# Settled engine orders, one more chunk in token order, and a shorter TensorE warm-up in a two-layer linear-attention kernel

## The chip, the cores and the metric

The kernel runs on one core of one Trainium2 chip. The metric is the device time of one execution in microseconds (us); smaller is better. A profile comes from one execution whose span (first to last instruction) is some 1.7 us shorter than the device time of the same run.

## The reference, cut to what matters

Two identical layers, each an attention block A and an MLP block B, over 2048 tokens of width 512; 32 heads of 16; hidden width 1792; everything in bf16.

```python
def _A_ref(x, wqkv, wo):                       # x: (1, 2048, 512)
    qkv = (x @ wqkv) ...                       # split in q, k, v by heads
    phi = lambda t: jnp.where(t > 0, t + 1, jnp.exp(t)) + 1e-6
    pq, pk = phi(q), phi(k)
    kv  = einsum("bhsd,bhse->bhde", pk, v)     # sums over ALL tokens
    z   = einsum("bhsd->bhd", pk)              # sums over ALL tokens
    num = einsum("bhqd,bhde->bhqe", pq, kv)
    den = einsum("bhqd,bhd->bhq", pq, z)[..., None] + 1e-6
    return (num / den) ... @ wo

x = x + _A_ref(_layernorm(x), wqkv, wo);  x = x + _B_ref(_layernorm(x), w1, b1, w2, b2)
x = x + _A_ref(_layernorm(x), wqkv, wo);  x = x + _B_ref(_layernorm(x), w1, b1, w2, b2)   # [cut]
```

What matters: kv and z need every token, so each layer has a **join** at which nothing of the attention's output can start until the last phi(k) has been summed. The kernel hides it behind Q tiles and behind the other block.

## The kernel before

The kernel is a list of named operations. Each has an engine, a modelled duration, the data that it reads and writes, and the buffers ("tiles") that it takes. A scheduler in the kernel file puts the operations of each engine in one order when the kernel is built; the engine's program holds them in that order, and semaphores do the waiting.

The names used below: `K0_9` is the K tile of token tile 9 in layer 0 (the code counts layers from 0, the text of the prediction from 1), `Q0_1_2` a Q tile of chunk 1 (four token tiles make a chunk), `G` the sums of phi(k) with the normed input y, from which the kv product is made, `Z` the sums of phi(k), `D` the denominator matmul, `KV`, `M` the products at the join, `WO` the attention's output, `PTA` a transpose on TensorE, `TA` one by DMA; `stats`, `aggr`, `veps`, `pow`, `norm` are the steps of a layer norm (`pow` on POOL), `exp`, `relu`, `min`, `phi` those of phi.

Before, the order came out of priorities. Among the operations that could start soon, the one with the smallest number went first:

```python
def run(self):                                       # class Scheduler, before
    ...                                              # [cut]
        for o in released[e]:
            at = max(o.ready, t0)
            pr = o.prio
            if o.table is not None and o.table != table:     # [shortened]
                at = max(o.ready, t0 + TABLE_LOAD)
                pr += self.table_penalty
            ...                                      # [cut: a free buffer or bank?]
            if at <= t0 + self.window ...:           # the best priority among those that start soon
                if soon is None or (pr, at, o.seq) < soon[:3]:
                    soon = (pr, at, o.seq, o)
    ...
CONF = dict(N_K=4, N_Q=2, ..., TABLE_PENALTY=25.46, WINDOW=126.58,
    SHIFT={"B00_0": -359.6, "B00_1": -532.9, ...,    # [cut: some 260 tuned numbers]
           "phik0_2": 27.1, "phik1_8": 23.4, ...},
    WAY={..., "den0_2": "tok", "den1_2": "tok", "den1_3": "tok", ...})   # free choices
```

The kernel uses PSUM (the memory that TensorE writes to) as eight banks of 128x512 fp32. They are given out by the same scheduler, by its modelled times: whichever allowed bank is free first is taken.

```python
def take(self, t):                                   # class Banks
    _, b = min(self.options(t))                      # earliest free bank, in modelled time
```

The denominators of a chunk can be made in two ways. In the usual one TensorE multiplies phi(q) with a block matrix `zb`, ACT takes Ln and Exp (a reciprocal), and DVE or POOL multiplies. In the **token form** Q comes out with tokens on the partitions; DVE or POOL multiplies by z, DVE sums over each head's 16 columns and takes the reciprocal, and a DMA transpose turns the result round:

```python
if by_token(L, c):                                   # WAY["den{L}_{c}"] == "tok"
    for k in range(4):
        G.op("pool" or "dve", ... tensor_tensor(lr, tok(), zrow, mult) ...)      # pz
        G.op("dve",  ... tensor_reduce(rd, heads(lr), X, ADD) ...)               # red
        G.op("dve",  ... rd + 1e-6 ...)                                          # den
        G.op("dve",  ... reciprocal(rr, rd) ...)                                 # rec
        G.op("pool" or "dve", ... tok() * rr ...)                                # pr
        dma("sp", ... dma_start_transpose(...))                                  # TP
    return pt
for kt in range(DT):
    G.op("pe",  ... matmul(bank(b), lhsT=zb[...], rhs=pq[:, kt, :]) ...)         # D
    G.op("act", ... Ln, then Exp(scale=-1) ...)                                  # ln, rec
    G.op("pool" or "dve", ... pq * lr ...)                                       # pr
```

The warm-up keeps TensorE busy while the first input arrives:

```python
def warm(e):
    for _ in range(11):
        ins = e.matmul(bank(wu), lhsT=onesm[:, 0:P], rhs=onesm[:, :], start=True, stop=True)
    return ins
```

Of the kernel before, what the change touches and what calls it, by code (L numbers as in the profile page):

```python
# [22 lines left out]
ENGINES = ("pe", "act", "dve", "pool", "sp")  # L23
# [29 lines left out]
class Op:  # L53
    __slots__ = ("eng", "fn", "dur", "lat", "deps", "tiles", "prio", "name", "table", "sem", "nbytes",
                 "idx", "start", "end", "ready", "missing", "outs", "waits", "tok", "opens", "seq", "fast", "n", "grp", "soft")

    def __init__(self, eng, fn, dur, lat, prio, name, table=None, sem=None, nbytes=0, fast=False, n=1):
# [6 lines left out]

        self.soft = []
# [47 lines left out]
class Scheduler:  # L113


    def __init__(self, graph, psum, table_penalty=4.0, window=60.0):
        self.g = graph
        self.psum = psum
        self.table_penalty = table_penalty
        self.window = window  # L120
# [6 lines left out]
    def run(self):  # L127
        g = self.g
        for o in g.ops:
            o.soft = [d for d in o.soft if d not in o.deps]  # L130
            o.missing = len(o.deps) + len(o.soft)
        for o in g.ops:
            for d in [*o.deps, *o.soft]:
                d.outs.append(o)
        released = {e: [] for e in ENGINES}
        for o in g.ops:
            if o.missing == 0:
                released[o.eng].append(o)
# [6 lines left out]
        left = len(g.ops)  # L145
        while left:
            best = None
            for e in ENGINES:
                cand = None
                t0 = free[e]  # L150
                soon, late = None, None
                for o in released[e]:
                    at = max(o.ready, t0)
                    pr = o.prio
                    if o.table is not None and table is not None and o.table != table:
                        at = max(o.ready, t0 + TABLE_LOAD)
                        pr += self.table_penalty
                    ok = True
                    for t in o.tiles:
                        if t.slot is None:  # L160
                            s = self.slot_time(t)
                            if s is None:
                                ok = False
                                break
                            if s > at:
                                at = s
                    if not ok:
                        continue
                    if at <= t0 + self.window or (o.table is not None and at <= t0 + TABLE_LOAD + self.window and o.table != table):
                        if soon is None or (pr, at, o.seq) < soon[:3]:  # L170
                            soon = (pr, at, o.seq, o)
                    if late is None or (at, pr, o.seq) < late[:3]:
                        late = (at, pr, o.seq, o)
                if soon is not None:
                    cand = (soon[1], soon[0], soon[3])
                elif late is not None:
                    cand = (late[0], late[1], late[3])
                if cand is not None and (best is None or cand[:2] < best[:2]):
                    best = cand
            if best is None:  # L180
                raise RuntimeError("no operation can start: " + str(
                    [(e, [o.name for o in released[e]][:6]) for e in ENGINES]))
            at, _, o = best
# [30 lines left out]
            released[e].remove(o)  # L214
            left -= 1
# [4 lines left out]
            for w in o.outs:  # L220
                w.missing -= 1
                if o not in w.soft:
                    w.ready = max(w.ready, o.end + self.latency(o, w))
                if w.missing == 0:
                    released[w.eng].append(w)
# [70 lines left out]
def assign_waits(graph, order, sems, dma_sems):  # L296
# [10 lines left out]
    while len(done) < total:  # L307
# [45 lines left out]
    N_HALF=1, N_K=4, N_Q=2, P_Z0=0.37, N_PB=1, N_PT=8, P_DEN=-3.16, P_A2=-51.68, P_W1=-4.93, P_W2=79.13,  # L353
    P_K=87.88, P_G=146.7, P_Q=46.72, STEP=1.68, A1_Q=81.1, A1_STEP=4.54, N_H=2, N_N=2, GAP=0,
    TABLE_PENALTY=25.46, WINDOW=126.58,
    SHIFT={
        "B00_0": -359.6, "B00_1": -532.9, "B00_2": 40.9, "B00_3": 41.9, "B01": 316.2, "B02": 368.2,
        "B03": 123.2, "B10_0": -153.5, "B10_1": -88.2, "B10_2": 8.8, "B10_3": 74.2, "B11": 335.0,
        "B12": 293.5, "B13": -86.9, "D00": -322.6, "D01": -51.3, "D02": -123.2, "D03": 13.2, "D10": 4.8,
        "D11": -31.4, "D12": -41.2, "D13": 102.5, "G00_0": -22.1, "G00_1": -11.3, "G00_2": 110.8,  # L360
        "G00_3": 221.9, "G01_0": -39.6, "G01_1": 112.5, "G01_2": -42.7, "G01_3": -305.4, "G02_0": 213.7,
        "G02_1": -30.8, "G02_2": 606.6, "G03_0": -23.0, "G03_1": -78.8, "G03_3": -25.3, "G0_2_0": 12.2,
        "G10": -239.1, "G11": 116.2, "G12": 664.9, "G13": -18.0, "G1_1_0": -8.3, "G1_3_0": 17.0, "K00_0": 1.2,
# [98 lines left out]
def build_kernel(nc, A_x, A_wqkv, A_wo, B_x, B_w1, B_b1, B_w2, B_b2, out, conf=None, report=False):  # L462
# [5 lines left out]
    with ExitStack() as es:  # L468
# [131 lines left out]
        def warm(e):  # L600
            for _ in range(11):
                ins = e.matmul(bank(wu), lhsT=onesm[:, 0:P], rhs=onesm[:, :], start=True, stop=True)
            return ins
# [629 lines left out]
```

## Time and profile before

| | before |
|---|---|
| device time, median of the first 3 runs | 334.51 us (333.75 to 335.18) |
| span of the profiled run | 332.2 us |
| TensorE busy | 324.7 us |
| DVE, ACT, POOL busy | 219.1, 208.7, 146.8 us |
| TensorE gaps and late clock after 1.5 us | about 6.3 us |

A busy TensorE hides small gaps, so the useful measure is the distance from the start of one matmul to the next, less what the same shape takes in the steady part (the prediction below works these distances out). Whatever is above that is a **gap**. All gaps in this document are made in this way, and single ones under 0.1 us are mostly left out.

### The profile page before, as it was taken

What the parts mean: (1) busy time and instruction counts of PE and PEld (TensorE: products, weight loads), DVE (VectorE), ACT (ScalarE), POOL (GpSimd) and SP (SyncE); (2) the same over time, 40 slices, a digit from 0 to 9 for tenths busy, and PEclk for the clock granted to TensorE, in tenths of its full rate; (3) what the DMA queues carried; (4) which work ended last, traced back from release to release, by engine and by line L of the source; (5) the groups of instructions that cost most, each with busy time, mean ns of one, the idle gap of its engine ahead of it and who ended that gap; (6) DMA issues with size and microseconds to landing.
All of it is one profiled execution on the core that took longest, in us unless ns stands there. A gap on an engine that the chain in (4) does not pass through costs nothing.

```text
span 332.2 us, 4772 instructions
## 1 busy us (share of the span) xinstructions
PE 324.7 (98%) x1735; PEld 159.6 (48%) x1735; DVE 219.1 (66%) x461; ACT 208.7 (63%) x348; POOL 146.8 (44%) x238
## 2 busy tenths in 40 slices
PE   7999899999999999999999999999999999999996
PEld 3444444487444444444444444448744444444444
DVE  6988669996974593060777889998898585520022
ACT  2988499598989739374562286979956501735600
POOL 5883415768862938020359400284793062120000
DMA  7745750122030102122010110001152122201011
GB/s 264 258 76 83 258 190 0 34 47 49 17 79 2 33 0 39 26 47 49 16 32 3 32 33 2 0 17 34 39 116 69 32 66 64 47 15 35 0 40 57
DMA packets 42836, 19.07 MB, mean 57 GB/s; under 512 B 36476, under 2 KB 41852, under 8 KB 42812
## 3 DMA queue, kind: packets, MB, share of 16 engines
q1 hardware_dynamic: 39244, 11.55, 16.1%
q0 software_dynamic: 1056, 4.72, 4.0%
q10 hardware_dynamic: 2512, 2.49, 2.3%
q8 instruction: 14, 0.23, 0.3%
q14 instruction: 10, 0.08, 0.1%
HBM read 8.00 MB, written 2.10 MB: 30 GB/s over the span
## 4 chain that ended last, share of the span: by engine, by line
PE 78%; DVE 9%; DMA 5%; POOL 4%; ACT 3%; issue 1%; DVEq 0%; POOLq 0%
PE ps L1030 27%; PE ps L992 26%; PE ps L960 8%; PE ps L717 4%; PE ps L748 3%; PE ps L844 3%; DMA t<-yb 3%; PE ps L735 2%; PE ps L812 2%; POOL rstd L630 2%; DMA b1t<-b1r 1%; DVE gtb L828 1%; DVE yb L643 1%; DVE stats L618 1%; DMA t<-in_A_x_dram 1%; PE ps L936 1%
## 5 line engine op out<-in xcount | busy, mean ns | idle before, releaser
L998 ACT ACTIVATE gT<-ps,b1c 128x512 bf16<-128x512 f32 (+1 forms) x140 | 81.0, 601 | 46.0 <-PE ps L992 40.3
L992 PE MATMUL ps<-t,w 128*128 128x512 bf16 (+1 forms) x560 | 99.3, 337 | 0.4 <-ACT t L676 0.4
L1030 PE MATMUL ps<-w,gT 128*128 128x512 bf16 x434 | 97.3, 379 | 0.0
L992 PEld LDWEIGHTS ps<-t,w 128*128 128x128 bf16 x560 | 54.5, 98 | 44.0 <-ACT t L676 1.5
L1030 PEld LDWEIGHTS ps<-w,gT 128*128 128x128 bf16 x434 | 42.3, 98 | 50.4
L687 ACT ACTIVATE eb<-ps 128x512 bf16<-128x512 f32 x64 | 37.9, 604 | 14.7 <-PE ps L717 7.1
L630 POOL TENSOR_TENSOR rstd<-veps,neghalf 128x1 f32<-128x1 f32 x64 | 38.3, 601 | 6.9 <-DVE veps L628 2.1
L638 ACT ACTIVATE yb<-xsb,nmr,rstd 128x512 bf16<-128x512 f32 x25 | 19.6, 808 | 25.2 <-POOL nmr L635 22.6
L618 DVE BATCH_NORM_STATS2 stats<-xsb 128x6 f32<-128x512 f32 x48 | 32.8, 682 | 0.8
L717 PE MATMUL ps<-wqkv,t 128*128 128x512 bf16 x128 | 30.9, 380 | 1.2 <-DMA t<-yb 0.7
L960 PE MATMUL ps<-gtb,t 128*128 128x512 bf16 x128 | 31.4, 380 | 0.2 <-DVE gtb L828 0.2
L1040 DVE TENSOR_TENSOR outb<-ps,xsb 128x512 bf16<-128x512 f32 x15 | 10.2, 682 | 29.3 <-PE ps L1030 29.3
L944 POOL TENSOR_TENSOR t<-t,lr 128x512 bf16<-128x512 bf16 x10 | 11.6, 1163 | 36.4 <-ACT lr L940 36.4
L623 POOL TENSOR_SCALAR veps<-mv 128x1 f32<-128x1 f32 x32 | 8.8, 274 | 41.2 <-DVE mv L620 39.5
L698 ACT ACTIVATE rb<-ps 128x512 bf16<-128x512 f32 x41 | 24.8, 609 | 3.3 <-PE ps L748 2.3
L1036 DVE TENSOR_TENSOR xsb<-ps,xsb 128x512 f32<-128x512 f32 x16 | 10.7, 675 | 23.7 <-PE ps L1030 23.7
L977 POOL TENSOR_TENSOR xsb<-xsb,b2b 128x512 f32<-128x512 f32 x19 | 22.5, 1192 | 3.1 <-DVE yb L643 2.0
L700 DVE TENSOR_SCALAR eb<-eb 128x512 bf16<-128x512 bf16 x41 | 15.1, 378 | 11.2 <-ACT eb L687 11.1
L628 POOL TENSOR_SCALAR veps<-mv 128x1 f32<-128x1 f32 x29 | 7.4, 257 | 32.8 <-DVE mv L620 31.5
L717 PEld LDWEIGHTS ps<-wqkv,t 128*128 128x128 bf16 x128 | 11.9, 97 | 16.2 <-ACT t L676 0.9
L748 PE MATMUL ps<-t,wqkv 128*128 128x512 bf16 x80 | 19.6, 379 | 0.0
L960 PEld LDWEIGHTS ps<-gtb,t 128*128 128x128 bf16 x128 | 12.3, 98 | 15.2 <-DVE gtb L828 1.2
(91 smaller groups left out, 402.3 us busy)
## 6 DMA issues: line engine op xcount, KB each, us to landing
w<-in_B_w_dram POOLq DMA_DIRECT2D x4, 896.0 KB, 8.4
out_dram<-outb SPq DMA_DIRECT2D x15, 128.0 KB, 1.7
t<-in_A_x_dram ACTq DMA_DIRECT2D x3, 512.0 KB, 8.2
t<-yb SPq DMA_TRANSPOSE x54, 2.4
wqkv<-in_A_wqkv_dram SPq DMA_DIRECT2D x1, 512.0 KB, 5.5
wqkv<-in_A_wqkv_dram ACTq DMA_DIRECT2D x1, 512.0 KB, 7.2
wqkv<-in_A_wqkv_dram POOLq DMA_DIRECT2D x1, 512.0 KB, 6.2
wo<-in_A_wo_dram POOLq DMA_DIRECT2D x1, 512.0 KB, 5.6
```

The source lines that it names most:

```text
L618: G.op("dve", lambda e: e.bn_stats(stats[:, s.slot, :], src()), 620, reads=src_keys, writes=[k + "s"], tiles=[s, *src_tiles], prio=prio, n ...
L630: G.op("pool", lambda e: e.tensor_tensor(rstd[:, s.slot:s.slot + 1], veps[:, s.slot:s.slot + 1], neghalf[:], op=ALU.pow), 570, reads=[k + ...
L638: G.op("act", lambda e: e.activation(yb[:, y.slot, :], src(), ACT.Identity, bias=nmr[:, s.slot:s.slot + 1], scale=rstd[:, s.slot:s.slot + 1]),
L687: G.op("act", lambda e: e.activation(eb[:, et.slot, :], bank(bt), ACT.Exp), 478, reads=[src_key], writes=[f"e{tag}"], tiles=[bt, et], prio ...
L698: G.op("act", lambda e: e.activation(rb[:, rt.slot, :], bank(bt), ACT.Relu), 478, reads=[src_key], writes=[f"r{tag}"], tiles=[bt, rt], pri ...
L717: ins = e.matmul(bank(b), lhsT=yTa(yT)[:, dt, k * P:(k + 1) * P], rhs=wqkv[:, dt, D:2 * D], start=(dt == 0), stop=(dt == DT - 1))
L748: ins = e.matmul(bank(b), lhsT=wqkv[:, dt, kt * P:(kt + 1) * P], rhs=yTa(yT)[:, dt, :], start=(dt == 0), stop=(dt == DT - 1))
L960: ins = e.matmul(bank(wb), lhsT=yTa(pq)[:, kt, k * P:(k + 1) * P], rhs=gtb[:, kt, :], start=(kt == 0), stop=(kt == DT - 1))
L977: G.op("pool" if on_pool else "dve", lambda e: e.tensor_tensor(xsb[:, st, :], xsb[:, st, :], b2b[:], op=ALU.add), 1120 if on_pool else 600 ...
L992: ins = e.matmul(bank(b, n), lhsT=w1[:, dt, ft * P:(ft + 1) * P], rhs=yTa(yT)[:, dt, k0 * P:k1 * P], start=(dt == 0), stop=(dt == DT - 1))
L998: G.op("act", lambda e, ft=ft, b=b, k0=k0, k1=k1, n=n: e.activation(gT[:, g.slot, ft * 512 + k0 * P:ft * 512 + k1 * P], bank(b, n), ACT.Ge ...
L1030: ins = e.matmul(bank(b), lhsT=gT[:, g.slot, ft * 512 + k * P:ft * 512 + (k + 1) * P], rhs=w2[:, ft, :], start=(ft == 0), stop=(ft == FT - 1))
```

## The change

The intent: a priority moves an operation past everything else of the same engine, and one changed number can shuffle much of the program. The changed kernel keeps each engine's order as a list that is settled by moving one operation at a time. The scheduler only gives out buffers, banks and semaphores. Along with it came the token form for layer 1's chunk 1, a shorter warm-up, other limits on PSUM banks and other free choices.

```diff
-ENGINES = ("pe", "act", "dve", "pool", "sp")
+ENGINES = ("sp", "pe", "act", "dve", "pool")
 ...
 def run(self):
-    released = {e: [] for e in ENGINES}
     ... [cut]
+    queue = {e: [by_name[n] for n in self.named[e].split()] for e in ENGINES}
             for e in ENGINES:
-                for o in released[e]:
-                    ... [cut: priority, table penalty, window]
+                if len(self.order[e]) == len(queue[e]):
+                    continue
+                o = queue[e][len(self.order[e])]         # the head of the list, no choice
+                if o.missing:
+                    continue
 ...
-    N_HALF=1, N_K=4, N_Q=2, ... N_H=2, N_N=2, GAP=0,
-    TABLE_PENALTY=25.46, WINDOW=126.58,
-    SHIFT={ ... },
+    N_HALF=1, N_K=4, N_Q=3, ... N_H=4, N_N=2, GAP=28.61,
+    ORDER={
+        "pe":
+            "warm PTA0_0 PTA0_1 K0_0 K0_1 PTA0_2 PTA0_4 K0_2 G0_0_0 PTA0_3 K0_4 K0_3 Q0_0_0 G0_1_0 PTA0_5 G0_2_0 Q0_0_1 K0_5 "
+            ... [cut: five lists]
+    },
     WAY={ ...
+        "den1_1": "tok",
         ... [cut: other choices, among them 8 bias additions from POOL to DVE]
 def warm(e):
-    for _ in range(11):
-        ins = e.matmul(bank(wu), lhsT=onesm[:, 0:P], rhs=onesm[:, :], start=True, stop=True)
+    for n in [D] * 9 + [P]:
+        ins = e.matmul(bank(wu, n), lhsT=onesm[:, 0:P], rhs=onesm[:, 0:n], start=True, stop=True)
 ... [cut: names for operations without one, small changes of modelled durations, soft dependencies of layer 1's norms, phi(k) and G taken out]
```

## The prediction

> **What bounds the kernel now.** I read the page's busy times first, then the chain that ended last, then the TensorE timeline row by row, and last the list of TensorE's waits. Busy times, and the row of 40 slices:
>
> ```profile
> PE 324.7 (98%) x1735; PEld 159.6 (48%) x1735; DVE 219.1 (66%) x461; ACT 208.7 (63%) x348; POOL 146.8 (44%) x238
> ...
> PE   7999899999999999999999999999999999999996
> ...
> PE 78%; DVE 9%; DMA 5%; POOL 4%; ACT 3%; issue 1%; DVEq 0%; POOLq 0%
> ```
>
> TensorE is filled from the first slices to the last; no other engine passes two thirds. The third line, the chain's shares, says the same: where DVE, DMA or POOL appear in it, they are what TensorE stood waiting for. But a busy TensorE is not one without gaps, since a matmul's record (379 ns) overlaps the next. So I took start-to-start distances. In the steady part they are very even:
>
> ```profile
> 226.76 11.35 PE ps L992 x104
> 238.12 12.09 PE ps L1030 x56
> 250.20 12.09 PE ps L992 x56
> ```
>
> These are pieces of the chain of waits: 12.09/56 = 0.216 us for a matmul of 512 columns, 11.35/104 = 0.109 us for 256. One of 128 columns takes 0.056 us, one of a single column 0.025 us, from the same kind of distances. Summed over the 1735 matmuls of the trace, with the warm-up's eleven at the 0.427 us that they really took, the work is 321.6 us. The span of 332.2 us is then 1.5 us before the first matmul, 321.6 us of work, about 6.3 us of gaps and late clock, and 2.8 us from the start of the last matmul to the end. Those 6.3 us are all that better order alone can win. Where they lie shows in the TensorE timeline (start, length, what; the bracket is idle time and what ended it):
>
> ```profile
> 1.51 4.87 PE L602 MATMUL ps<-onesm 128*128 128x512 bf16 x11 [1.51 <-DVE onesm L566]
> 6.18 1.06 PE L666 MATMUL ps<-idp,yb 128*128 128x128 bf16 x8
> 7.50 1.90 PE L717 MATMUL ps<-wqkv,t 128*128 128x512 bf16 x8 [0.26 <-ACT t L676]
> 9.23 0.39 PE L666 MATMUL ps<-idp,yb 128*128 128x128 bf16 x4
> 10.20 0.40 PE L666 MATMUL ps<-idp,yb 128*128 128x128 bf16 x4 [0.58 <-DVE yb L643]
> 10.69 1.04 PE L717 MATMUL ps<-wqkv,t 128*128 128x512 bf16 x4
> ...
> 23.84 1.02 PE L717 MATMUL ps<-wqkv,t 128*128 128x512 bf16 x4 [0.40 <-DMA t<-yb]
> ...
> 40.31 0.55 PE L793 MATMUL ps<-onesm,pkb 128*128 128x1 bf16 x16 [0.84 <-DVE pkb L704]
> ...
> 85.34 1.04 PE L992 MATMUL ps<-t,w 128*128 128x512 bf16 x4 [0.41 <-ACT t L676]
> ...
> 198.28 1.04 PE L717 MATMUL ps<-wqkv,t 128*128 128x512 bf16 x4 [0.33 <-DMA t<-yb]
> ...
> 214.91 1.25 PE L960 MATMUL ps<-gtb,t 128*128 128x512 bf16 x5 [0.21 <-DVE gtb L828]
> ```
>
> By start distances over those ideal ones, the gaps are: 1.9 us between 6.2 and 11 us (transposes and first K tiles, DVE-paced), 1.0 us at 15 to 24 us (the larger part a wait for a DMA transpose), 1.0 us at 39 us (the sum of phi(k) waits for DVE), 0.6 us at 42 to 56 us (the kv product and its copies), 0.6 us at 84.6 us, 0.5 us at 197.6 us (again a DMA transpose), 0.6 us at 204 to 215 us. From 216 us to the last matmul there is none: the second half of the last layer cannot get shorter by order.
>
> **What the Trainium skill says.** "TensorE: Matmul & The Clock Gate", section "Wait — 56ns, not 53.3ns?", gives start-to-start 426.7 ns at 512 columns cold and 215.7 ns warm, 106.7 and 55.6 ns at 128. The trace agrees: the warm-up matmuls start 0.427 us apart, the first four transposes 0.107, from 6.84 us on 0.056, and the first K tile 0.216. Same page, section "What's actually happening": the clock is released by activity in a free-running window of about 3.4 us, so the moment varies. Here it fell between 6.5 and 6.9 us; one trace cannot show the spread. "ScalarE: Activation LUTs", section "What ACT_TABLE_LOAD costs", gives about 1283 ns a load; the 14 loads here measure 1283. "GPSIMD Engine Reference", section "Engine selection", puts elementwise work on it at roughly half VectorE's speed; here the phi sums take 1214 ns on POOL and 422 on DVE, so moves between these two are not neutral.
>
> **The change, part by part.** I counted the instructions of both built programs.
>
> Removed from TensorE: one and three quarter warm-up matmuls (11 of 512 columns become 9 of 512 and one of 128): 2 x 0.427 - 0.107 = 0.75 us of cold time. Whether the path gets it is another matter (below). Four denominator matmuls of layer 2's second chunk, 4 x 0.216 = 0.86 us. One group of four TensorE transposes, 4 x 0.056 = 0.22 us. K, Q, attention, MLP matmuls are equal in number; the token form of Q swaps its operands only. The last two, 1.1 us, come off an engine that is the bound, so all of it counts, if nothing takes its place.
>
> Added elsewhere by the token form: 4 each of reduce (0.675), add (0.360), reciprocal (0.339) and four products with z and with the reciprocal on DVE or POOL (0.75 to 1.25), and 4 DMA transposes (2.4 us to landing); gone are 4 Ln (0.689) and 4 Exp (0.636) on ACT. The new assignment of free choices moves more: eight bias additions from POOL to DVE (+6.0, -9.5 us), five fewer norms on ACT, four more relus, two more table loads (+2.6 us). By these rows' durations ACT falls by some 3 us, DVE rises by some 6 to 225 us, POOL by 3.5 to 150. All stay under 70% of the span, so none of this is on the path except where TensorE waits.
>
> The head, worked by hand from measured durations. Now the first norm runs on DVE from 5.01 to 5.42 us, and its transpose waits for the warm-up until 6.18. A warm-up shorter by 0.75 ends at 5.43, when the norm is just done. But DVE's new order puts the third tile's statistics (0.68) and the second's aggregate (0.18) ahead of the first norm: 5.05 + 0.68 + 0.2 = 5.93, norm to 6.34, first transpose at 6.40. The second norm comes behind statistics 3 and aggregate 2: to 7.86, its transposes 7.92 to 8.14, the first K tile at 8.16 against 7.50 now. The two K tiles end at 9.9; the next transposes (tiles 2 and 4) are ready at 9.4 and 10.5; the copy of the first of these, behind exp and relu on ACT, ends near 10.75, and K of tile 2 starts near 10.85 against 10.69 now. As many transposes and K tiles are done by then in both. So the shorter warm-up gains nothing: the head comes out at +0.2 us.
>
> The later gaps. At 15 to 24 us the new order has Q tiles of two token-form chunks between the K tiles. From K of tile 2 to K of tile 7, the first fed by a DMA transpose, lie nine groups of 0.86 us: it is reached near 19 us, and its transpose should land by 17.4. I count 0.9 of the 1.0 us won. At 39 us the last z sum of layer 1 had 2.1 us of work between it and the last K tile and waited 1.0; it now has two Qs, one G and one z sum, 3.0 us: 0.8 won. The kv join keeps its shape; at most 0.1. At 84.6 us the first MLP's second half no longer sits on late copies: 0.6 won. At 197 us the last K tile has 11 us of work behind the MLP's end, about as now; 0.2 won. The second kv join still sends its four copies ahead of layer 2's first output tile: 0.1.
>
> Sum: -0.86 - 0.22 + 0.2 - 0.9 - 0.8 - 0.1 - 0.6 - 0.2 - 0.1 = -3.6 us. In-order queues always add a few new small waits; I give back 0.3. 334.5 - 3.3 = 331.2 us, 1.0% faster.
>
> **The rivals.** First, the late clock. With the warm-up over near 5.4 us and idle time until 6.4 and again until 7.9, the window that released the clock may not be filled. Then the first two K tiles run cold, 8 x 0.211 = 1.7 us more, and some of what follows. Against: 3.9 us of busy time is more than one window. For: the window runs free, and the trace shows the clock still half at 6.5 us, after 5.0 us of work. This makes it 332 to 333.5 us. Second, the order closes nearly all gaps: 6.3 - 0.5 and 1.1 of work, 327.7 us. For: order settled by single moves may be fitted to the chip. Against: the head is DVE-paced and the joins wait on real chains. Third, new waits: fixed queues, and DVE with 6 us more in the joins, where it is already filled (23.2 of 26.0 us from 190 to 216 us). The lines are
>
> ```profile
> 190.00:216.00 26.00, 25.47 (x142) 11.62 (x141) 23.18 (x52) 20.74 (x38) 2.58 (x4) 1.00 0.05 11
> 216.00:262.00 46.00, 46.00 (x273) 26.30 (x272) 39.37 (x77) 35.39 (x62) 29.07 (x39) 1.00 0.25 55
> ```
>
> (window, length, then busy time and count of PE, PEld, DVE, ACT, POOL, then clock, DMA share, GB/s). That would leave about 334 us.
>
> **Range and chances.** 2% faster would be under 327.9 us: 6.6 us of the at most 6.3 + 1.1 that are to be had, so 0.06. Slower by 2% would need 6.7 us of new gaps on a tuned order: 0.01. Within 2%: 0.93. The range of 8 in 10 runs from 328.7 (rival two, in part) to 333.6 us (rival one).
>
> **What would show it.** Right: the first K tile at about 8.2 us and the third near 10.9; no wait on a DMA transpose near 23 us; 16 matmuls with zb in place of 20; no gap in TensorE from 60 to 190 us; still under 1 us of gaps in each join. Wrong: the first transpose before 6 us (then the head gains), K tiles 0.427 us apart after 8 us (rival one), TensorE waits over 1 us between 60 and 330 us (rival three), or fewer than 2 us of gaps in all (rival two).

## More of the kernel before

One trap: in five of the fourteen traces every fiftieth or so matmul record is missing, which looks like a gap of exactly one matmul; the weight load of the missing one is there, and such gaps are taken out.

## The result, and the profile after

| | before | after |
|---|---|---|
| device time, median (lowest to highest) | 334.02 us (333.69 to 335.18), 5 runs | 330.14 us (330.07 to 330.16), 5 runs |
| span of the profiled run | 332.2 us | 328.4 us |
| DVE busy | 219.1 us | 211.9 us |
| ACT busy | 208.7 us | 202.1 us |
| POOL busy | 146.8 us | 146.8 us |
| matmuls with `zb` | 20 | 16 |

The ratio is 0.9877, with a 95% interval of 0.9858 to 0.9896: 1.2% faster, within 2%. (A ratio is the mean time of one kernel's fast runs over that of the other's of the same rounds, so it is not quite the ratio of the medians quoted.) The kernel before took 334.0 to 335.2 us from one group of runs to the next, so runs of different groups are best compared by ratios.

The page of the changed kernel, busy times, TensorE's row of 40 slices and the shares of the chain that ended last:

```profile
PE 320.1 (97%) x1696; PEld 159.1 (48%) x1726; DVE 211.9 (65%) x475; ACT 202.1 (62%) x343; POOL 146.8 (45%) x237
...
PE   6899999999999999999999999999999999999996
...
PE 90%; DVE 3%; ACT 2%; DMA 2%; issue 1%; POOL 0%
```

TensorE is still the only full engine. The chain's share of TensorE went from 78 to 90%; DVE's fell from 9 to 3, DMA's from 5 to 2, POOL's from 4 to 0. These shares show where TensorE waited for others, not for how long: 12 points of the span are some 39 us, and only 3.8 were won. (1696 records against 1726 weight loads: 30 matmul records are missing in this trace.)

TensorE's timeline of the changed kernel (start, length, what; bracket: idle time and what ended it):

```profile
1.51 4.13 PE L655 MATMUL ps<-onesm 128*128 128x512 bf16 x10 [1.51 <-DVE onesm L619]
6.02 0.40 PE L719 MATMUL ps<-idp,yb 128*128 128x128 bf16 x4 [0.38 <-DVE veps L681]
7.16 0.40 PE L719 MATMUL ps<-idp,yb 128*128 128x128 bf16 x4 [0.74 <-DVE veps L681]
7.40 1.89 PE L770 MATMUL ps<-wqkv,t 128*128 128x512 bf16 x8
...
10.82 1.03 PE L770 MATMUL ps<-wqkv,t 128*128 128x512 bf16 x4
...
38.69 0.54 PE L846 MATMUL ps<-onesm,pkb 128*128 128x1 bf16 x16
...
200.13 0.39 PE L934 MATMUL ps<-dz,onesm 128*128 128x512 bf16 x1 [0.21 <-DVE dz L931]
...
205.56 0.40 PE L920 MATMUL ps<-gtb,wqkv 128*128 128x128 bf16 x4
...
212.83 1.47 PE L1013 MATMUL ps<-gtb,t 128*128 128x512 bf16 x6 [0.17 <-DVE gtb L881]
```

Here the reader is to see four things. The warm-up now ends at 5.6 us, but the first transposes wait for DVE until 6.02 and the next until 7.16: the time that the warm-up gave up has become waiting. Eight K matmuls in 1.89 us are 0.216 apart, so the clock was up by 7.4 us. The last z sum of layer 0, at 38.69, has no bracket any more, where it waited for DVE before. And the last three lines lie in the second join, where TensorE now waits more than before.

The list of TensorE's waits after, without the warm-up's own (total, times, longest, in us):

```profile
PE ps L719 <- DVE veps L681: 1.1, 2, 0.7
PE ps L719 <- DVE yb L696: 0.9, 2, 0.7
PE ps L934 <- DVE dz L931: 0.2, 1, 0.2
PE ps L1013 <- DVE gtb L881: 0.2, 1, 0.2
```

Two of the four lines are transposes in the first 11 us, two are the second join. The waits for the z sum, for the DMA transposes and for the MLP's copies, that stood in the list before, are gone. By regions, gaps before and after:

| region | before, us | after, us |
|---|---|---|
| first 11 us (transposes and first K tiles, from the end of the warm-up) | 1.9 | 2.8 |
| 12 to 36 us (K and Q tiles, DMA transposes) | 1.04 | 0.32 |
| 39 us (last z sum, layer 0) | 1.0 | 0 |
| 41 to 57 us (first join) | 0.64 | 0.11 |
| 84.6 us (first MLP) | 0.57 | 0 |
| 197 us (last K tile fed by DMA) | 0.49 | 0 |
| 199 to 215 us (second join) | 0.63 | 1.20 |
| 216 us to the end | 0 | 0.03 |

The gaps fell by 1.9 us with these figures; the matmuls taken out are 0.75 (warm-up), 0.86 (`zb`) and 0.22 us (transposes). Together that is 3.7, and the span fell by 3.8. The change altered orders, banks and free choices at once. Below, the warm-up (runs 1 to 3), the place of the z sum (runs 4 and 5) and the matmuls of the second join (run 7) are tested alone; for the regions at 12 to 36, 41 to 57, 84.6 and 197 us no run tells whether the order, the banks or the choices closed the gap.

### The profile page after: what moved, and what is told of

Read it like the earlier page. It is cut to its first block, busy times and chain, and to the rows that moved or that the text cites. A ratio compares the mean times of both kernels' runs of the same rounds, so it can differ in the third digit from the quotient of the medians.

```text
span 328.4 us, 4737 instructions
## 1 busy us (share of the span) xinstructions
PE 320.1 (97%) x1696; PEld 159.1 (48%) x1726; DVE 211.9 (65%) x475; ACT 202.1 (62%) x343; POOL 146.8 (45%) x237
## 4 chain that ended last, share of the span: by engine, by line
PE 90%; DVE 3%; ACT 2%; DMA 2%; issue 1%; POOL 0%
PE ps L1045 29%; PE ps L1083 28%; PE ps L1013 8%; PE ps L770 8%; PE ps L865 4%; PE ps L801 4%; PE ps L788 3%; PE ps L897 2%; DMA t<-in_A_x_dram 2%; PE ps L1070 1%; PE ps L989 1%; ACT eb L740 1%; DVE gtb L910 1%; PE ps L719 1%; PE ps L846 0%
## 5 line engine op out<-in xcount | busy, mean ns | idle before, releaser
L1051 ACT ACTIVATE gT<-ps,b1c 128x512 bf16<-128x512 f32 (+1 forms) x140 | 76.9, 601 | 56.9 <-PE ps L1045 53.0
L1045 PE MATMUL ps<-t,w 128*128 128x512 bf16 (+1 forms) x552 | 101.2, 336 | 0.3
L740 ACT ACTIVATE eb<-ps 128x512 bf16<-128x512 f32 x64 | 36.9, 602 | 8.4 <-PE ps L770 4.5
L683 POOL TENSOR_TENSOR rstd<-veps,neghalf 128x1 f32<-128x1 f32 x64 | 37.1, 585 | 6.5 <-DVE veps L681 3.0
L751 ACT ACTIVATE rb<-ps 128x512 bf16<-128x512 f32 x45 | 26.6, 605 | 7.5 <-PE ps L770 3.9
L691 ACT ACTIVATE yb<-xsb,nmr,rstd 128x512 bf16<-128x512 f32 x21 | 16.9, 810 | 16.0 <-POOL nmr L688 15.9
L757 POOL TENSOR_TENSOR t<-eb,rb 128x512 bf16<-128x512 bf16 x14 | 16.8, 1201 | 12.2 <-DVE eb L753 7.5
L696 DVE TENSOR_SCALAR yb<-xsb,mv,rstd 128x512 bf16<-128x512 f32 x27 | 15.5, 578 | 8.8 <-POOL rstd L683 8.6
L997 POOL TENSOR_TENSOR t<-t,lr 128x512 bf16<-128x512 bf16 x13 | 15.3, 1180 | 12.7 <-ACT lr L993 12.3
L681 POOL TENSOR_SCALAR veps<-mv 128x1 f32<-128x1 f32 x29 | 8.0, 279 | 27.6 <-DVE mv L673 26.9
```

Of the source, the lines that this page charges most:

```text
L683: G.op("pool", lambda e: e.tensor_tensor(rstd[:, s.slot:s.slot + 1], veps[:, s.slot:s.slot + 1], neghalf[:], op=ALU.pow), 570, reads=[k + ...
L691: G.op("act", lambda e: e.activation(yb[:, y.slot, :], src(), ACT.Identity, bias=nmr[:, s.slot:s.slot + 1], scale=rstd[:, s.slot:s.slot + 1]),
L740: G.op("act", lambda e: e.activation(eb[:, et.slot, :], bank(bt), ACT.Exp), 478, reads=[src_key], writes=[f"e{tag}"], tiles=[bt, et], prio ...
L751: G.op("act", lambda e: e.activation(rb[:, rt.slot, :], bank(bt), ACT.Relu), 478, reads=[src_key], writes=[f"r{tag}"], tiles=[bt, rt], pri ...
L757: lambda e: e.tensor_tensor(dst(), eb[:, et.slot, :], rb[:, rt.slot, :], op=ALU.add),
L1045: ins = e.matmul(bank(b, n), lhsT=w1[:, dt, ft * P:(ft + 1) * P], rhs=yTa(yT)[:, dt, k0 * P:k1 * P], start=(dt == 0), stop=(dt == DT - 1))
```

## The experiments

Line numbers differ between the runs, since tables of orders and banks were put into the kernel file.

### 1 to 3: the warm-up alone

The changed kernel with 11, and with 4, warm-up matmuls of 512 columns, and the kernel before with the shorter warm-up. All orders and banks are as in the kernel that each starts from.

```diff
-    for n in [D] * 9 + [P]:
+    for n in [D] * 11:          # second run: [D] * 4
```

> The changed kernel with the warm-up put back to eleven matmuls of 512 columns; every order as it is. Theory (the head is paced by VectorE, the shorter warm-up gains nothing): the warm-up then ends at 1.51 + 11 x 0.427 = 6.2 us, the first transpose moves from 6.02 to 6.2, the second transpose stays at 7.16 because its norm is not ready before, and the time stays within 0.2 us of the changed kernel's 330.1. Rival (the 0.75 us of warm-up are on the path): 330.9.

> The changed kernel with only four warm-up matmuls. They end at 3.2 us, and TensorE then stands idle until the first norm. Theory (the length matters only for the clock): the clock is not released, the first K tiles run at 0.427 us a matmul, and the time rises by 1 to 3 us, to 331 to 333. Rival (length is a plain cost, and the clock does not need it): 330.1 or less.

> The kernel before with the shorter warm-up alone (9 of 512 columns and one of 128), its orders untouched. Theory: its first norm is ready at 5.42 us, so the first transpose comes at about 5.5 in place of 6.18, but the second waits for its norm at 6.8 as before; the first K tile moves from 7.5 to about 7.1, the third only from 10.7 to about 10.5: 0.2 us at most, within the noise of the kernel before (333.7 to 335.2). Rival: the whole 0.75 us. If the clock is released later, slower by 1 us or more.

| run | device time, us | ratio to before | span |
|---|---|---|---|
| 11 matmuls | 330.38 (330.11 to 330.55) | 0.9863 [0.9834, 0.9892] | 328.6 |
| 4 matmuls | 331.31 (330.93 to 331.40) | 0.9889 [0.9860, 0.9919] | 329.2 |
| before, shorter warm-up | 334.45 (333.66 to 335.42) | 0.9987 [0.9947, 1.0026] | 333.2 |

With 11 matmuls the first transposes start at 6.18, the first K at 7.50 and the third at 11.21 us, against 6.02, 7.40 and 10.82. The span is 0.2 us longer and the ratio no worse: the 0.75 us taken from the warm-up bought some 0.2 at most, as the prediction had it. (The later third K says little: in the six traces with the changed kernel's head it starts anywhere from 10.79 to 11.19.) With 4 matmuls the clock comes late. TensorE's timelines of the run with 4, then of the kernel before with the shorter warm-up:

```profile
5.79 0.61 PE L719 MATMUL ps<-idp,yb 128*128 128x128 bf16 x4 [2.39 <-DVE veps L681]
...
7.33 3.47 PE L770 MATMUL ps<-wqkv,t 128*128 128x512 bf16 x8
```

```profile
6.84 0.61 PE L666 MATMUL ps<-idp,yb 128*128 128x128 bf16 x4 [0.75 <-DVE yb L643]
7.24 3.62 PE L717 MATMUL ps<-wqkv,t 128*128 128x512 bf16 x8
```

Eight K matmuls in 3.5 us, 0.427 apart, are the cold clock: 1.7 us more for them. (The granted clock reads 1.00 there, from 8 to 10 us in both runs, so it doesn't show this cold start; the spacing of the matmuls does.) So rival one of the prediction exists. It cost the run with 4 matmuls about 1 us net. The kernel before with the shorter warm-up also started its K tiles at the cold clock in its profiled run, although its warm-up is that of the changed kernel. One trace doesn't tell how often that happens; in the changed kernel the clock was up at the first K tile in both profiled runs and in the seven of the runs below that keep its warm-up, and its five first times lie within 0.1 us.

### 4: the z sum moved back

To test the 39 us term, the last z sum was put where it had less work ahead of it, right behind the last K tile.

```diff
-"K0_11 K0_9 Q0_1_1 G0_8_0 Z0_3 Q0_0_2 Z0_2 G0_9_0 Q0_0_3 ..."
+"K0_11 K0_9 Z0_2 Q0_1_1 G0_8_0 Z0_3 Q0_0_2 G0_9_0 Q0_0_3 ..."
```

> The changed kernel with one operation moved on TensorE alone: the z sum of layer 1's third chunk stands right behind the last K tile, in place of four groups later. Theory (the gain at 39 us is filler put between a producer and its consumer): the sum needs the phi that VectorE ends at 38.35 us, would stand at 35.7, so TensorE waits 2.7 us there and the time rises by 2.2 to 2.7 us, to 332.3 to 332.8. Rival (the order of single operations matters little, later slack takes it up): under 0.5 us.

Measured: 337.25 us (336.17 to 337.82), ratio 1.0075 [1.0036, 1.0113], span 334.4. One moved operation made the changed kernel slower than the kernel before. The wait is there:

```profile
38.50 0.55 PE L846 MATMUL ps<-onesm,pkb 128*128 128x1 bf16 x16 [2.54 <-DVE pkb L757]
```

A wait of 2.7 us was expected and 2.54 came; but the span rose by 6.0. The other part lies elsewhere: 3.1 us of gaps from 66 to 91 us, where TensorE waits for ACT's gelu. The built programs say why: 58 of the 330 PSUM tiles had changed their bank. With the z sum earlier in modelled time, another bank was free first, a Q tile went into a bank that the MLP tiles use, and they were left with three of four. So this run moved two things, and another was needed.

### 5: the same with the banks held

```diff
+PIN = {tile name: bank in the changed kernel, ...}      # all 330 tiles
-        for b in allowed:
+        for b in ((PIN[t.name],) if t.name in PIN else allowed):
```

> The same single move as in the run before (the z sum right behind the last K tile), with every PSUM bank held to the one that the changed kernel gives it. In the run before, the time rose by 7 us and not by 2.7: the trace showed the 2.7 us wait, and then some 3 us of waits on gelu from 66 to 90 us, and 58 of 330 tiles had other banks, since banks are given out by the modelled times. Theory (the further 3 us come from the banks): with the banks held, only the wait of 2.7 us stays, 332.6 to 333.0. Rival (a late group makes all later queues late): 335 or more.

Measured: 334.81 us (334.41 to 335.18), ratio 1.0002 [0.9987, 1.0017], span 333.5. No gap from 66 to 91 us is left, so the banks had cost about 3 us: the two executions of the run before whose mean granted clock was also 0.995 took 337.8 us. But 334.8 is 1.8 us above the range of 332.6 to 333.0 that was expected, and just below the rival's 335. Busy times by stretch (window, length, busy time and count of PE, PEld, DVE, ACT, POOL, then the granted clock, DMA share and GB/s):

```profile
38.00:40.00 2.00, 0.81 (x18) 0.61 (x19) 1.29 (x5) 0.00 (x0) 0.23 (x1) 1.00 0.93 358
40.00:42.00 2.00, 2.00 (x10) 0.81 (x9) 0.00 (x0) 0.00 (x0) 0.00 (x0) 0.69 1.02 423
42.00:44.00 2.00, 1.76 (x20) 0.91 (x20) 0.16 (x1) 0.00 (x0) 0.00 (x0) 0.50 1.00 367
```

The granted clock falls to 0.5: after a wait of 2.54 us (2.70 from start to start) TensorE was throttled again, and matmuls from 40.7 to 44.3 us stand 0.427 apart. That is 1.7 us which neither theory nor rival had. The Trainium skill, "TensorE: Matmul & The Clock Gate", section "What's actually happening", has the clock go cold after at least one idle window of about 3.4 us. This run throttled after a shorter wait, so a wait of 2.5 us must be counted with the clock that it may cost. In the profiled execution without pins, the same wait of 2.54 us did not throttle. The mean granted clocks tell how often it does: without pins two of four executions have 0.995 (337.8 us, against 336.2 and 336.7 for those at 1.0), with pins all four have 0.994 or 0.995.

### 6: the token form under the old scheduler

```diff
-        "den0_2": "tok", "den1_2": "tok", ...
+        "den0_2": "tok", "den1_1": "tok", "den1_2": "tok", ...      # kernel before, priorities as they were
```

> The kernel before with layer 2's second chunk in token order too, alone; its scheduler settles the orders again by its priorities. Theory (the form itself saves 4 x 0.216 = 0.86 us of TensorE work, and the rest depends on the order that the priorities happen to give): 333 to 336, so not clearly better. Rival (the form alone is a gain of 1 us or more through ScalarE's eight activations less): 333.3 or less.

Measured: 348.76 us (347.65 to 351.27), ratio 1.0444 [1.0401, 1.0487]. The waits of TensorE:

```profile
PE ps L666 <- ACT yb L638: 4.3, 1, 4.3
PE ps L1030 <- ACT gT L998: 2.2, 1, 2.2
```

The form takes four matmuls off TensorE, and the kernel got 14 us slower, which neither theory nor rival had. These two waits are not at the denominators: the priorities, tuned for another program, settled the order anew. Nearly all of it lies behind 215 us, with 14.8 us of gaps; of these some 3.1 are again the half clock, after the wait of 4.3 us and after that of 2.2 (0.50 from 253 to 256 us). In a build, the old scheduler could not place the program at all ("no operation can start") when the warm-up's modelled duration was shortened, so in run 3 that was left as it was. This shows why orders were made into lists: with lists a part can be changed and the order of the rest stays. It doesn't show what the token form is worth by itself under a good order; that stays with the count of matmuls and the next run.

### 7: four denominator matmuls put back in the second join

Each of the four D matmuls of layer 1's chunk 0 runs twice (the result is the same), which adds 0.86 us of TensorE work just where the token form took 0.86 away.

```diff
+reps = 2 if (L, c) == (1, 0) else 1
-ins = e.matmul(bank(b), lhsT=zb[...], rhs=yTa(pq)[:, kt, :], ...)
+for _ in range(reps): ins = e.matmul(bank(b), lhsT=zb[...], rhs=yTa(pq)[:, kt, :], ...)
```

> The changed kernel with each of the four denominator matmuls of layer 2's first chunk done twice into the same bank; orders and banks as they are. It adds 4 x 0.216 = 0.86 us of TensorE work in the second join, as much as the token form of the second chunk took away. Theory (TensorE's work is the path there): +0.7 to +0.9 us, 330.8 to 331.0. Rival (the join from 199 to 213 us is paced by VectorE, and TensorE's 1.2 us of gaps take it up): under +0.3 us.

Measured: 330.79 us (330.39 to 331.35), ratio 0.9883 [0.9868, 0.9898], span 328.5 against 328.4. The gaps of the second join fell from 1.20 to 0.65 us: 0.55 of the 0.86 us of work went into gaps that were there anyway. That leaves 0.3 us; the span rose by 0.1 only because a wait of 0.2 us at 28.4 us is absent in this trace. By the ratios (0.9883 against 0.9877 and 0.9871) the whole costs 0.2 to 0.4 us, but their intervals are wider than that, so the trace decides. It speaks for the rival: in the join, taking out a matmul was worth less than half its time.

### 8: the head, first try

In the first 11 us DVE sets the pace. Here each norm goes ahead of the next tile's statistics. Later banks are pinned.

```diff
 dve:  -"statsA0_1 statsA0_2 aggrA0_1 normA0_0 vepsA0_1 statsA0_3 aggrA0_2 normA0_1 ..."
       +"statsA0_1 normA0_0 aggrA0_1 vepsA0_1 statsA0_2 normA0_1 aggrA0_2 vepsA0_2 ..."
 pool: the two weight loads (wv, wo) behind the powers of tiles 3 and 4
 pe, act: tile 3 ahead of tile 4
```

> The changed kernel with its head put in the order of the data: each norm ahead of the next tile's statistics on VectorE, the weight loads of GpSimd behind the first five reciprocal roots, tile 3 ahead of tile 4 on TensorE and ScalarE; banks from layer 1's third chunk on held. Theory (the 2.9 us of gaps from 5.4 to 12.7 us are VectorE's and GpSimd's order): first K tile at 6.9 in place of 7.4 us, third near 9.7 in place of 10.8, time 1.0 us lower or more, 328.9 to 329.3. Rival (the head is paced by the landing of the inputs and the weights, or later waits on DMA transposes take the gain back): within 0.3 us of 330.1.

Measured: 331.87 us (331.33 to 332.07), ratio 0.9912 [0.9897, 0.9927], span 330.3. TensorE's timeline:

```profile
9.95 1.03 PE L810 MATMUL ps<-wqkv,t 128*128 128x512 bf16 x4
...
14.56 0.81 PE L905 MATMUL ps<-pkb,yb 128*128 128x512 bf16 x3 [1.64 <-DVE mv L713]
```

The third K tile starts 0.87 us earlier (9.95 for 10.82), as expected, and 1.6 us are lost at once at 12.7 us (the record of the second G's first matmul is missing; by its weight load it started at 14.34): the second G waits for a phi(k) that stands on DVE behind five statistics, two of them begun when its inputs were ready (12.70 to 13.96 us). The head can be made shorter, but DVE has to do something later for it.

### 9: the control

> The changed kernel once more, unaltered, as the control of this group on the same chip. If the earlier times of it carry over: 330.0 to 330.4 us, ratio to the kernel before 0.986 to 0.990, span near 328.4 us, TensorE gaps of 2.9 us in the head and 1.2 us at the second kv join. If this chip differs from the one that gave 330.14, it shows here, and the other two runs of the group are read against this one.

The changed kernel unaltered in the group of runs 10 and 11: 330.58 us (330.03 to 331.17), ratio 0.9871 [0.9840, 0.9901], span 328.5, the gaps of the second join again 1.20 us. The result carries over to another group.

### 10: the head, second try

```diff
 dve:  phik0_1 directly behind mink0_1; statsA0_7 aggrA0_7 earlier (tile 7 is the first to be transposed by DMA)
 pool: -"powA0_1 wv powA0_2 vepsA0_4 powA0_4 wo ..."
       +"... powA0_4 vepsA0_7 powA0_7 nmrA0_7 vepsA0_5 powA0_5 wv vepsA0_6 powA0_6 vepsA0_8 powA0_8 nmrA0_8 wo"
```

> The changed kernel with another order in the first 15 us alone: on DVE each norm goes ahead of the next tile's statistics, phi(k) of the second tile no longer stands behind four statistics, the statistics of the tile that is first transposed by DMA come earlier; on POOL the two weight loads are issued after the powers; PE takes K of tile 3 before tile 4's. The later PSUM banks are pinned to those of the changed kernel, so nothing else moves. Theory (DVE and POOL order sets the head, the first attempt failed only for phi(k) of the second tile): first K at about 7.1 us, third at 9.95, no gap over 0.3 us from 10 to 24 us, 0.8 to 1.0 us less in the span: 329.1 to 329.5 us. Rival (the DMA transposes, about 1.7 us apart once they start, set the pace up to 30 us, so an earlier start of K is lost at the first tiles fed by them): the third K is just as early, but a wait for a DMA transpose of 0.5 to 0.9 us stands between 18 and 26 us, and the time is 330.0 to 330.4 us.

Measured: 333.56 us (333.33 to 334.60), ratio 0.9965 [0.9932, 0.9998], span 331.8: 3.3 us longer than the control. The third K at 9.91 us, nothing lost at 12.7 us, but then (TensorE's timeline, and its busy time by stretch):

```profile
23.00 1.59 PE L810 MATMUL ps<-wqkv,t 128*128 128x512 bf16 x4 [2.46 <-DMA t<-yb]
```

```profile
24.00:25.00 1.00, 1.00 (x4) 0.40 (x3) 0.00 (x0) 0.37 (x1) 0.65 (x3) 0.50 0.00 0
```

A DMA transpose holds up a K tile for 2.5 us, and the wait again halves the clock (0.50). The clock is the smaller part of the loss: the one execution whose mean clock stayed at 1.0 took 333.33 us, the five others 333.44 to 334.60. The rival had named the transposes, for 0.5 to 0.9 us. The transfers show why it was so much. The DMA views of this run from 13 to 24 us, then of the first try from 14 to 24 us (median us from issue to landing):

```profile
t<-yb SPq DMA_TRANSPOSE x5, 4.3
```

```profile
t<-yb SPq DMA_TRANSPOSE x5, 2.5
```

In the second try the loads of wv and wo were issued at 13.9 and 17.1 us and landed at 18.9 and 21.7, just among the first transposes, which took 4.3, 5.5 and 4.8 us for the usual 2.5. In the first try they were issued at 10.0 and 11.0 and landed by 16.2. Nothing reads these weights before the first join: I had moved them because nobody waits for them, and they came into the way of what somebody does wait for.

### 11: the second join

The phi(q) product that POOL makes beside `zb` goes to DVE; `den1_1_0` goes behind the copy that the first KV product waits for; a Q tile goes ahead of the first D.

```diff
 pool: -"phik1_15 phiq1_0_2 pz1_1_0"          +"phik1_15 pz1_1_0"
 dve:  -"dz1 gt1_1 phiq1_0_1"                 +"dz1 gt1_1 phiq1_0_2 phiq1_0_1"
       -"ga1_2_0 den1_1_0 gt1_0 red1_1_1"     +"ga1_2_0 gt1_0 den1_1_0 red1_1_1"
 pe:   -"G1_2_2 D1_0_0 ZR1 ..."               +"G1_2_2 Q1_3_0 D1_0_0 ZR1 ..."
```

> The changed kernel with the second kv join alone altered: the phi(q) product that ran on POOL beside zb goes to DVE, the denominator addition goes behind the copy that the first kv product waits for, and a Q tile goes ahead of the first denominator matmul on PE; later banks pinned. Theory (zb took 1.46 us in place of about 0.7 because POOL worked beside it, and with the two denominator operations ahead of the copy this is where 1.20 us of gaps at 199 to 213 us come from): zb under 0.8 us, the gaps 0.4 to 0.8 us, 0.4 to 0.8 us less: 329.4 to 329.8 us. Rival (DVE is simply full there, and what goes to it from POOL pushes back the rest): zb is shorter, but the sum of the gaps stays 1.1 to 1.4 us and the time within 0.2 us of the unaltered kernel.

Measured: 331.52 us (331.35 to 332.53), ratio 0.9907 [0.9876, 0.9937], span 329.6, 1.1 us more than the control. The `zb` product in DVE's timeline of the changed kernel, then what POOL's timeline has beside it, then the same product in this run:

```profile
198.01 1.46 DVE L926 TENSOR_TENSOR zb<-bdmask,zs 128x512 bf16<-128x512 bf16 x1
```

```profile
197.77 1.15 POOL L757 TENSOR_TENSOR t<-eb,rb 128x512 bf16<-128x512 bf16 x1 [1.15 <-ACT rb L751]
```

```profile
197.87 0.69 DVE L966 TENSOR_TENSOR zb<-bdmask,zs 128x512 bf16<-128x512 bf16 x1
```

Half of the theory is shown: without the POOL product beside it `zb` takes 0.69 us for 1.46, as it did before the change, and the gaps at 199 us (0.63) and 205 us (0.24) are gone (the Q tile put ahead of D may have a share in the first). The Trainium skill, "GPSIMD Engine Reference", section "1. Specifications", has POOL share its SBUF interfaces with VectorE, with contention for DVE instructions in a 2-port mode or with two SBUF inputs; `zb` has two, and the trace agrees. But now (DVE's timeline, then ACT's):

```profile
205.13 1.15 DVE L1011 TENSOR_SCALAR rd<-rd 128x32 f32<-128x32 f32 x1
```

```profile
206.91 0.69 ACT L1031 ACTIVATE lr<-ps,eps 128x512 f32<-128x512 f32 x1 [1.90 <-DVE rd L1008]
```

`den1_1_0`, moved behind the copy, met POOL there: 1.15 us for 32 columns. How long such an addition takes is set by POOL: in this run and the changed kernel five of them (0.68 to 1.15 us) end 0.03 to 0.04 us after the POOL product beside them, and one with POOL idle takes 0.11. The reduction behind it came 0.8 us later, ACT waited 1.9 us for it (by the program, the reduction frees the buffer that ACT's Ln writes), and from 207 to 214 us TensorE had 2.6 us of gaps. Three things were changed at once here; the trace tells them apart for `zb` and for `den1_1_0`. The gap at 213.4 us (0.65) fits a bank: the builds' bank lists show that an output tile there was given the bank of a Q tile instead of that of a product already copied. No run tested that.

### 12: the head, third try

The weight loads early again, and the order and banks of layer 0's attention refitted around the new head by moving single operations, each kept if the kernel's own modelled times got no longer; in these the result was 0.7 us shorter than the changed kernel.

```diff
 pool: -"... powA0_5 wv vepsA0_6 powA0_6 vepsA0_8 powA0_8 nmrA0_8 wo"          (second try)
       +"powA0_0 id1 powA0_1 powA0_2 b1z vepsA0_3 powA0_3 wv vepsA0_4 powA0_4 wo vepsA0_7 powA0_7 ..."
 pe:   +"warm PTA0_0 PTA0_1 K0_0 PTA0_2 K0_1 PTA0_3 K0_2 G0_0_0 PTA0_4 K0_3 G0_1_0 K0_4 PTA0_5 Q0_0_0 ..."
 [cut: moves up to 60 us on all engines; 41 PSUM tiles in other banks]
```

> The head of the last but one try once more, with the one thing that its trace shows as its fault put right: the two weight loads on POOL are issued early again (behind the powers of the third and fourth tile on POOL, near 9 to 11 us), so that they have landed before the bulk of the DMA transposes. Each norm still goes ahead of the next tile's statistics, and phi(k) of the second tile is early. Behind it the order and PSUM banks of the first layer's attention are refitted by moving single operations, the later banks pinned to those of the changed kernel. Theory (the weight loads slowed the transposes, and those held K up): first K at about 7.1 us, third at about 9.9, DMA transposes 2.4 to 3.3 us to landing where the failed try had 4.3 to 5.5, no TensorE wait over 0.5 us from 11 to 36 us, clock not halved; ratio to the kernel before 0.983 to 0.986, some 0.5 to 1.0 us below the unaltered changed kernel (whose ratio was 0.987 to 0.988), span 327.4 to 328.0 us. Rival (whatever the head wins is given back by 36 us, since DVE and ACT are full there): third K as early, but new waits of 0.8 us or more in sum between 11 and 45 us, and a ratio of 0.987 or above, span 328.3 us or more.

Measured: 331.53 us (331.35 to 332.32), ratio 0.9903 [0.9884, 0.9921], span 329.6. The first K tile starts at 7.13 us, the third at 9.82, and the gaps of the first 11 us are 1.9 us, where the control has 3.1. That much of the head is really to be had. But the time is 1.1 us longer in the span. TensorE's timeline:

```profile
23.36 1.89 PE L813 MATMUL ps<-wqkv,t 128*128 128x512 bf16 x8 [1.08 <-DMA t<-yb]
```

One wait for a DMA transpose takes 1.2 us, and 0.9 us come at the first join (42 and 50 us). The rival had it right. This transpose was issued at 18.89 us and landed 4.33 us later, with the weight loads long landed (15.6 us). The DMA view of 18.5 to 23.5 us:

```profile
q1 hardware_dynamic: 1087, 0.26, 49.2%
q8 instruction: 1, 0.02, 1.8%
```

A single packet of the instruction queue q8, 0.02 MB, passes in that time. I looked for it in five traces. Each has one such packet between 14 and 32 us, and in four of them a transpose of about 4 us is in flight with it: 4.2 us in the kernel before (issued at 25.8), 4.0 in the changed kernel (24.3), 3.9 in the second try (27.2, apart from those beside the weight loads), 4.3 here; in the first try the transpose beside it took 2.9. The nine other traces fit: in four (runs 3, 4, 6, 9) a transpose of 3.9 to 4.3 us is in flight with the packet, in five (1, 2, 5, 7, 11) only ones of 2.4 to 3.2; and in none of the fourteen does a transpose of `yb` before 36 us take more than 3.6 us without this packet or the two weight loads beside it. That it is the fetch that slows the transpose is inferred from this coincidence and was not tested. In the changed kernel it costs 0.2 us, at 28.4 us, since the transpose concerned is not the next one that TensorE needs; in runs 1, 7 and 11, where the transposes there took 2.4 to 3.2 us, this wait is absent.

## Why the prediction was right

The predicted time of 331.2 us was 1.1 us above the measured 330.14, inside its range, and the class was right. Half of the 1.1 us is the starting point: 334.5 was the median of three runs, five give 334.02. The rest is the sum. By its terms:

| term of the sum | predicted, us | measured, us |
|---|---|---|
| four `zb` matmuls | -0.86 | -0.86 |
| four transposes | -0.22 | -0.22 |
| head (by the third K tile, 10.69 to 10.82) | +0.2 | +0.13 |
| 15 to 24 us | -0.9 | -0.84 |
| 39 us | -0.8 | -1.0 |
| first join | -0.1 | -0.53 |
| 84.6 us | -0.6 | -0.57 |
| 197 us | -0.2 | -0.49 |
| second join | -0.1 | +0.57 |
| new small waits (12.7 us, and after 216 us) | +0.3 | +0.15 |
| sum | -3.3 | -3.7 |

The span fell by 3.8. Single terms missed by up to 0.67 us, in both directions; that the sum came so close is in part luck.

**Bound.** Right: TensorE stayed the bound, and only gaps and removed matmuls moved the time. One reading was too strong: that DVE, DMA and POOL in the chain's shares "are what TensorE stood waiting for". They made up 18% of the span, some 60 us, and TensorE's gaps were 6.3.

**The head.** Right in its conclusion: the shorter warm-up gains nothing because DVE's order sets the first transposes. Run 1 shows it: with 11 matmuls the ratio is no worse. The single times were off: the first K came at 7.40, not 8.16, since DVE's operations follow each other closer than their durations say (two statistics of 1.29 us in sum were one stretch, and the first norm began at 5.58 us, not 5.93, the second at 6.69, not 7.45). The transposes of the next two tiles, behind which the third K waits (0.33 and 0.90 us of gaps), then took back what was won. The third K, on which the step rested, came at 10.82 against 10.85.

**39 us and 15 to 24 us.** Right in size; the cause at 15 to 24 us was not tested. That work between the last K tile and the z sum is what pays for the z sum's wait is shown by runs 4 and 5, where taking this work away brought a wait of 2.54 us.

**The joins.** These two terms failed, in opposite directions. "The kv join keeps its shape; at most 0.1" was mis-sized: it measured 0.53. "The second kv join still sends its four copies ahead of layer 2's first output tile: 0.1" failed outright: gaps rose from 0.63 to 1.20 us. The runs put in its place: `zb` on DVE at 1.46 us beside a POOL product, and the token form's operations on DVE ahead of the copy that the KV product waits for. With it falls part of another sentence, that the 1.1 us of matmuls "come off an engine that is the bound, so all of it counts, if nothing takes its place". In the second join, where the kernel before has its eight D matmuls of layer 1 between 203.9 and 212.6 us, 0.86 us of work went away and 0.57 us of gaps came, and run 7 put 0.86 back for 0.1 to 0.4 us. Something did take its place.

**Engine loads.** DVE was to rise by 6 us to 225; it fell to 211.9, POOL stayed at 146.8 where 150 was predicted, and ACT fell by 6.6 us, not 3. I took the eight bias additions and the token form in full and missed the products that went the other way, t<-t,lr from 10 on DVE to 3 (four gone with the token form, three moved to POOL). Nothing on the path hung on it. The measured 1214 and 422 ns that the prediction sets beside the skill's "roughly half" are a factor of 2.9; the measurement decides.

**Rivals.** The late clock did not occur in the profiled runs of the changed kernel, but runs 2, 3, 5, 6 and 10 show it to be close: a shorter warm-up, or a wait of 2.2 us and more. The second rival (nearly all gaps close, 0.5 us left) did not come: 4.4 us are left, 2.8 of them in the first 11 us and 1.2 in the second join. Everywhere else it nearly held, with 0.5 us left of 3.7. The third (new waits) came true in the second join only.

**Its signs.** Of those named for being right, the third K tile, the DMA transposes, the 16 matmuls and the stretch from 60 to 190 us came true; the first K tile (7.40 for 8.2) and "under 1 us of gaps in each join" (1.20 in the second) did not.

**What more order can give.** I tried to win back the head (runs 8, 10, 12) and the second join (run 11), and none of the four beat the unaltered changed kernel. Each shortened the gaps that it was made for, and each lost more than that further on. The changed kernel is the best version that I have.

## What to carry to other kernels

Where one engine is full, count its start-to-start gaps by region before believing in any gain, and weigh work removed inside a region with gaps at less than its own time. When one operation of a settled order is moved, hold the PSUM banks fixed first, or the run measures the banks as well. And before moving a transfer that nobody waits for, look what else is in flight at its new place.

## What the Trainium skill lacked or had wrong

- "TensorE: Matmul & The Clock Gate" (sections "What's actually happening" and "Why this matters for your kernels"): it has the clock fall after an idle window of about 3.4 us and warns of gaps above 3 us. Here it fell to 0.50 after waits of 2.5 us in runs 5 and 10 and of 2.2 us in run 6, at a cost of about 1.7 us in run 5; a wait of 2.54 us, as in run 5, did not throttle in the profiled execution of run 4, and gaps of 1.2 and 1.6 us (runs 12 and 8) did not either.
- The same page, section "Part 4: PE-mode transpose", says that the full clock doesn't engage for transpose-mode. Here the transposes, recorded as matmuls, start 0.107 us apart before the clock is released (the first four of the kernel before) and 0.056 us apart after it, in both kernels. Whether they ran in that mode the record doesn't show, so this doesn't yet refute the sentence.
- "DMA: Bandwidth & Descriptors" has nothing on how long a transpose takes beside other transfers: mostly 2.4 to 2.5 us, 4.3 to 5.5 us beside two weight loads of 512 KB, and 3.9 to 4.3 us in eight of fourteen traces when an instruction packet of 0.02 MB passed (a coincidence, not tested).
- On none of the pages did I find that matmul records can be missing at regular distances: 30 of 1726 here, each fiftieth, which looks like a gap of one matmul.
